# Attention and MLP in one kernel: an empty step, three moved transposes and a copy on another engine

## The chip, the cores and the metric

The kernel runs on one core of a Trainium2 chip. The metric is the device time of one execution in microseconds (us). TensorE (PE) multiplies, with its weight loads listed apart (PEld); VectorE (DVE), ScalarE (ACT) and GpSimd (POOL) do the elementwise work; SyncE (SP) and POOL issue most DMAs. Each engine works through its own list of instructions in order and waits on semaphores for the others.

## The reference

```python
q_n, k_n = rmsnorm(q, g_q), rmsnorm(k, g_k)            # 8 batches x 12 heads x 448 x 64
scores = q_n @ k_n.T / sqrt(64)
attn = softmax(scores); out = attn @ v
x = out.transpose(0, 2, 1, 3).reshape(8, 448, 768)
xn = (x - mean) / sqrt(var + 1e-6) * g_ln
y = x + relu(xn @ w_ch1) @ w_ch2                       # 768 -> 3072 -> 768
```

## The kernel before

**Units and pairs.** Heads are taken two at a time: a pair is two heads of one batch, six pairs to a batch, 48 in all (p = 0 to 47). A unit is the one or two pairs whose queries and keys are loaded and prepared together. Batch 0 has units 0 to 3, every later batch three units of two pairs; units 4, 5 and 6 are batch 1, and unit 8 is the middle unit of batch 2 (pairs 14 and 15), unit 24 the last.

**Preparing a unit** (`pieces`, line 233 on) is a set of small steps with letters. For the keys: `a` squares k on ACT (line 259) into the buffer `khl`; `d` sums the squares on DVE (line 265); `i` multiplies k by the two gains on POOL, in place (line 279); `j` (`khi`) writes the high part of k, a float16 copy, into `khl` (line 285 on POOL for the units listed in `POOL_HI`, line 287 on ACT for the others); `k` (`klo`) writes the low part, k minus the high part, on DVE (line 290). For the queries: `c` squares (ACT), `e` sums (DVE), `l` scales to float16 (DVE, line 83), `m` duplicates. From unit 7 on, SP then transposes by DMA: `x` the keys into `kU` (line 306), `y` the first 384 queries into `qU` with three DMAs (line 312), `Y` the last 64 with two (line 318). `kU`, `qU`, `qn` and `khl` have two buffers, used by even and odd units.

**Attention of a pair.** `scores(p, i)` for i = 0 to 5 multiplies 128 keys with 448 queries into a PSUM bank (line 405), and ACT takes the exponential into a tile E (line 421), which frees the bank. i = 6 is the 64 keys left over in each head; from unit 5 on the leftovers of the unit's two pairs go together into two banks with four matmuls (line 411). From pair 13 on there are three such banks. `values(p, i)` multiplies E with v into `oA` (line 458, three matmuls) and `oB` (line 460). Both lie in one set of PSUM banks, so the values of a pair begin only when `evac_o` of the pair before has divided and copied `oA` and `oB` out: two reciprocals and the products on lines 475 and 480, all on DVE.

**The MLP of a batch** runs while the attention of the next one does. First the activations `xn` of a tile of 128 tokens (DVE, line 662) are transposed by DMA from SP (line 688, `xnT`; only batch 0 uses PE), then PE multiplies with w1 (line 796, tile psH), ACT applies the relu (line 799), DVE builds sums of h in float16 (line 802), and PE multiplies with w2 (line 819). Batch 0 has an MLP of its own (`first_mlp`), whose second product is line 728 (tile psC), ends with an addition on DVE (line 755) and is stored by SP (line 954).

**The order is written out.** A hand-made list `ORDER` covers the work up to the end of batch 0's attention. Behind it `attention()` makes a list of steps, seven for each pair (p, i): in a step come the preparation steps due there (`todo`, from the tables `EARLY`, `TRANS_AT` and `PLAN`), one score, and one value product of the pair before. A step in which nothing happens isn't kept. `TRANS_AT[8] = (84, 85, 91)` puts `x`, `y` and `Y` of unit 8 at steps 84, 85 and 91, and step 7p + i is that of pair p. For p = 48 there are only the values of pair 47, at i = 1 to 6 (i = 1 has two of them). `run_rest` walks through the MLP of batch b in chunks of six matmuls or three, and behind each half chunk it emits as many steps as keep the share of steps done equal to the share of the MLP's cost, until the steps of the batch's stretch (`mark`) are used up. Then it emits `ln_list` of the next batch one item for each chunk: A, N0, N1 (lines 656 and 662), X0, X1 (line 688), R, with the X items held back until ten chunks are left. Stores of batch 0 either go out where the addition is emitted (`store`) or are put on the list `late` and go out at the next call of `store_late`.

Of the kernel before, what the change touches and what calls it, by code (L numbers as in the profile page):

```python
# [18 lines left out]
B, H, S, D = 8, 12, 448, 64  # L19
DM, FF = 768, 3072  # L20
NDC, NFF = DM // 128, FF // 128
NPAIR = H // 2
# [2 lines left out]
PAIR_UNIT = [(u, w) for u, (_, _, m) in enumerate(UNITS) for w in range(m)]  # L25
UNIT_PAIR = [PAIR_UNIT.index((u, 0)) for u in range(len(UNITS))]
EXP_BIAS = -4.0
DVE_KG, POOL_HI, POOL_DUP, ACT_Q = (0, 6), (1, 2, 3, 4, 5, 6), (3, 4, 5, 6), (0, 2, 4, 5)
POOL_SQUARE, POOL_LO = ((2, 1), (4, 0), (6, 0)), (5, 6)


# [4 lines left out]
ORDER = """  # L36
# [55 lines left out]
class _Fast:  # L92
# [446 lines left out]

    def attention(self):  # L540

        n, nu, nb0, done = B * NPAIR, len(UNITS), NPAIR, set(ORDER)
        todo = {}
        for u in range(4, nu):
            p, m = UNIT_PAIR[u], UNITS[u][2]
            if u == 4:
                continue
            plan = [(7 * (p - 4) + x, y) for x, y in PLAN]
            if u in EARLY:
                st, e = EARLY[u]  # L550
                names = ["bai", "d", "c", "e", "j", "gz", "k", "l", "m"]
                if u > 7:
                    names = NAMES[u]
                plan = [(st + (e - st) * x // 9, y) for x, y in enumerate(names)]
                if u >= DMA_UNIT:
                    plan += zip(TRANS_AT[u], "xyY")
            for at, names in plan:
                if self.late_v(u):
                    names = names.replace("z", "")
                todo.setdefault(at, []).extend(  # L560
                    self.prep_ops(u)[y] for y in names if y + str(u) not in done)
                for y in set(names) & set("kl"):
                    x = u, "qk"[y == "k"]
                    i = RING.index(x) + 3 if x in RING else nu * 2
                    if i < len(RING):
                        todo.setdefault(at + (LOAD_AT[y == "l"] if u not in EARLY else 1), []).append(
                            lambda x=RING[i]: self.load_unit(x[0], ("qk".index(x[1]),)))
        for g, at in enumerate(W2_AT):
            todo.setdefault(at, []).append(lambda g=g: self.load_w2(g))
        steps, mark = [], [0]  # L570

        for p in range(nb0, n + 1):
            for i in range(7):
                c = []
                if i == 0 and p < n and p % NPAIR == 0 and p > nb0:
                    c.append(lambda b=p // NPAIR: self.batch(b))
                c += todo.pop(7 * p + i, [])
                if p < n and f"S{p}.{i}" not in done and i < 6:
                    c.append(lambda p=p, i=i: self.scores(p, i))
                if p > nb0:  # L580
                    for x in {0: (), 1: (0, 1)}.get(i, (i,)):
                        if f"V{p - 1}.{x}" not in done:
                            c.append(lambda p=p, x=x: self.values(p - 1, x))
                if p < n and i == 6 and f"S{p}.6" not in done:
                    c.append(lambda p=p: self.scores(p, 6))
                if p > nb0 + 1 and i == 1 and (p - 1) % NPAIR:
                    c.append(lambda p=p: self.stats(p - 2))
                if p + 1 < UNIT_PAIR[DMA_UNIT]:
                    if i == 2 and f"K{p + 1}" not in done:
                        c.append(lambda p=p: self.trans_k(p + 1))  # L590
                    if i == 4 and f"Q{p + 1}" not in done:
                        c.append(lambda p=p: self.trans_q(p + 1))
                if p > nb0 and p % NPAIR == 0 and i == 6:
                    c.append(lambda p=p: self.stats(p - 1))
                if c:
                    steps.append(c)
            if p > nb0 and p % NPAIR == 0:
                mark.append(len(steps))
        return steps, mark
# [108 lines left out]
    def first_mlp(self):  # L708

        nc, sh = self.nc, self.sh  # L710
        tiles, xnT, hT, cur = self.tok_tiles(0), self.xnT, self.hS, {}

        def up(f, i):
            if i == 0:
                cur["h"] = self.ps_m.tile([128, 512], FP32, tag="mlp", name="psH")
            ps = cur["h"]
            for dc in range(3 * i, 3 * i + 3):
                nc.tensor.matmul(ps[:, 0:384], sh.w1[:, dc, ts(f, 128)], xnT[:, dc],  # L718
                                 start=(dc == 0), stop=(dc == NDC - 1))
            if i:  # L720
                nc.scalar.activation(out=hT[:, f], in_=ps[:, 0:384], func=AFT.Relu)

        def down(t, g, s):
            if s == 0:
                cur["ps"] = self.ps_m.tile([128, 512], FP32, tag="mlp", name="psC")
            ps = cur["ps"][:, 0:HCOL]
            for f in range(3 * s, 3 * s + 3):
                nc.tensor.matmul(ps, hT[:, f, ts(t, 128)], sh.w2[:, f, ts(g, HCOL)],
                                 start=(f == 0), stop=(f == NFF - 1))
            if s == 7:  # L730
                self.add(0, t, g, ps)
                if g and t < 2:
                    self.late.append((0, t, slice(0, DM)))
                elif t == 2:
                    self.store(0, t, slice(g * HCOL, g * HCOL + HCOL))
            elif s == 3:
                self.store_late()

        for f in range(UP_FIRST, NFF):
            yield 6 * 384 / 2.4, [lambda f=f, i=i: up(f, i) for i in range(2)]  # L740
        for g in range(2):
            for t in range(3):
                for s in range(4):
                    yield 6 * HCOL / 2.4, [lambda t=t, g=g, s=s: down(t, g, s)
                                           for s in (2 * s, 2 * s + 1)]
# [228 lines left out]
    def run_rest(self):  # L974
        steps, mark, upto = self.steps, self.mark, self.upto
        for b in range(B):
            tail = TAIL[b]
            chunks = list(self.mlp_chunks(b))
            total = sum(c for c, _ in chunks)
            if b + 1 == B:  # L980
                for i, (_, emit) in enumerate(chunks):
                    if i == len(chunks) - 55:
                        self.tc.mark_branch_hint_location("general", "LikelyTaken", [ENG.PE, ENG.DVE, ENG.SP, ENG.Activation, ENG.Pool])
                    for call in emit if isinstance(emit, list) else [emit]:
                        call()
                    if i in FLAG_AT:
                        self.flag(FLAG_AT.index(i))
                break
            start, goal = self.pos, mark[b + 1]
            done, items = 0.0, None  # L990
            if b == 0:
                ops, last = self.weight_sums()
            elif b == 1:
                ops += last
            left = sum(c > 0 for c, _ in chunks)
            for cost, emit in chunks:
                if not cost:
                    emit()
                    continue
                for i, call in enumerate(emit):  # L1000
                    call()
                    if i + 1 < len(emit):
                        upto(int(min(goal, start + (goal - start) * (done + cost / 2) / (total - 960 * tail))))
                left -= 1
                if (left < 10 if b == 0 else b == 1) and ops:
                    ops.pop(0)()
                done += cost
                upto(int(min(goal, start + (goal - start) * done / (total - 960 * tail))))
                if self.pos >= goal:
                    if items is None:  # L1010
                        items = self.ln_list(b + 1)
                        for u, (x, _, _) in enumerate(UNITS):
                            if x == b + 2 and self.late_v(u):
                                self.ln[f"Z{u}"] = self.prep_ops(u)["z"]
                                items.append(f"Z{u}")
                    if items and (items[0][0] != "X" or left <= DOWN):
                        x = items.pop(0)
                        self.ln[x]()
            for x in items:
                self.ln[x]()  # L1020
            if b + 2 == B:
                upto(len(steps))
# [223 lines left out]
```

## Time and profile before

The median of three runs is 584.49 us (583.91 to 585.04). One further execution was profiled.

| | |
|---|---|
| profiled execution, its own time | 584.28 us |
| its span, first to last instruction | 582.7 us |
| busy: PE, DVE, ACT, POOL | 563.3, 379.9, 376.0, 190.4 us |
| share of the span: PE, DVE, ACT, POOL | 97%, 65%, 65%, 33% |

The profile page gives the busy time of each engine and its groups of instructions by source line. The trace behind it gives each instruction's start and duration in a timeline, where the bracket at the end of a row is the engine's idle time before it and what ended it. Matmuls are pipelined: one starts long before the end of the one in front of it, so a lost stretch of PE is read from the distance between starts, and the idle time in the bracket is the smaller figure. An instruction of SP that issues a DMA ends when the issue is done, not when the data have landed.

### The profile page before, as it was taken

What the parts mean: (1) busy time and instruction counts of PE and PEld (TensorE: products, weight loads), DVE (VectorE), ACT (ScalarE), POOL (GpSimd) and SP (SyncE); (2) the same over time, 40 slices, a digit from 0 to 9 for tenths busy, and PEclk for the clock granted to TensorE, in tenths of its full rate; (3) what the DMA queues carried; (4) which work ended last, traced back from release to release, by engine and by line L of the source; (5) the groups of instructions that cost most, each with busy time, mean ns of one, the idle gap of its engine ahead of it and who ended that gap; (6) DMA issues with size and microseconds to landing.
All of it is one profiled execution on the core that took longest, in us unless ns stands there. A gap on an engine that the chain in (4) does not pass through costs nothing.

```text
span 582.7 us, 13655 instructions
## 1 busy us (share of the span) xinstructions
PE 563.3 (97%) x5446; PEld 414.2 (71%) x5446; DVE 379.9 (65%) x826; ACT 376.0 (65%) x691; POOL 190.4 (33%) x207
## 2 busy tenths in 40 slices
PE   6888999999999999999999999999999999999996
PEld 4656666677686867777677867777687777778684
DVE  6989567699657566846667586854756733663424
ACT  4998787458774779558776588747787477323130
POOL 4885635303430711553240520653141410020000
PEclk9899999999999999999999999999999999999999
DMA  7999999959672966968573887958743490030201
GB/s 198 255 238 222 219 201 162 183 170 122 121 129 79 157 136 133 133 142 112 120 119 41 187 121 137 128 152 115 145 57 64 126 104 1 2 108 1 83 2 58
DMA packets 178329, 72.59 MB, mean 125 GB/s; under 512 B 138212, under 2 KB 173220, under 8 KB 178260
## 3 DMA queue, kind: packets, MB, share of 16 engines
q1 hardware_dynamic: 133876, 52.52, 43.5%
q0 software_dynamic: 43440, 18.52, 26.5%
q8 instruction: 44, 0.72, 0.5%
q10 hardware_dynamic: 944, 0.62, 0.4%
q14 instruction: 25, 0.20, 0.1%
HBM read 52.76 MB, written 11.01 MB: 109 GB/s over the span
## 4 chain that ended last, share of the span: by engine, by line
PE 78%; DVE 7%; DMA 5%; ACT 5%; issue 2%; SPq 2%; ACTq 0%; DVEq 0%
PE psH L796 32%; PE psP L819 28%; PE psS L405 7%; PE oA L458 4%; ACT E L421 3%; PE psH L718 2%; DMA q<-in_q_dram 2%; DMA w2s<-in_k_dram 1%; PE oB L460 1%; PE psS L411 1%; DVE ssq L265 1%; DVE stat L641 1%; DMA k<-in_k_dram 1%; ACT khl L259 1%; SPq L154 1%
## 5 line engine op out<-in xcount | busy, mean ns | idle before, releaser
L421 ACT ACTIVATE E<-psS,rr_all 128x448 f16<-128x448 f32 x336 | 203.7, 635 | 41.0 <-PE psS L405 36.9
L796 PE MATMUL psH<-xnT,w 128*128 128x256 f16 (+1 forms) x2016 | 225.8, 261 | 0.4 <-DMA xnT<-xn 0.4
L796 PEld LDWEIGHTS <-w 128*128 128x128 f16 x2016 | 172.6, 98 | 24.5 <-issue 4.7
L799 ACT ACTIVATE hS<-psH 128x512 f16<-128x512 f32 x150 | 90.1, 600 | 95.9 <-PE psH L796 91.9
L819 PEld LDWEIGHTS <-hS 128*128 128x128 f16 x1080 | 99.7, 98 | 58.2 <-DVE hS L802 1.5
L819 PE MATMUL psP<-w,hS 128*128 128x384 f16 x672 | 126.8, 326 | 0.0
L405 PE MATMUL psS<-qU,kU 128*128 128x448 f16 x288 | 101.4, 354 | 5.1 <-ACT E L421 3.3
L458 PEld LDWEIGHTS <-E 128*128 128x128 f16 x1008 | 70.5, 98 | 36.8 <-issue 3.0
L279 POOL TENSOR_TENSOR k<-k,gprod 128x896 f32<-128x896 f32 x18 | 38.3, 2128 | 148.1 <-ACT khl L259 131.6
L802 DVE TENSOR_TENSOR hS<-hS 128x512 f16<-128x512 f16 (+1 forms) x119 | 58.7, 500 | 22.3 <-ACT hS L799 20.8
L819 PE MATMUL psP<-w2s,hS 128*128 128x384 f16 (+1 forms) x408 | 70.2, 321 | 0.0
L458 PE MATMUL oA<-v,E 128*128 128x65 f16 x864 | 67.1, 193 | 1.5 <-DVE x L475 0.7
L755 DVE SCALAR_TENSOR_TENSOR x<-psP,rs_all,x 128x384 f32<-128x384 f32 x60 | 36.4, 617 | 41.8 <-PE psP L819 41.1
L460 PE MATMUL oB<-v,E 128*128 128x65 f16 x288 | 51.9, 193 | 0.3
L830 POOL TENSOR_TENSOR x<-x,hS 128x384 f32<-128x384 f32 x21 | 23.5, 1128 | 83.2 <-ACT hS L898 82.6
L216 POOL DMA_DIRECT2D v<-in_v_dram x54 | 41.4, 779 | 9.1 <-PE oB L460 8.1
L473 DVE RECIPROCAL rec_all<-oA 128x6 f32<-128x6 f32 x48 | 9.2, 192 | 46.9 <-PE oA L458 46.8
L290 DVE TENSOR_TENSOR khl<-k,khl 128x896 f16<-128x896 f32 x18 | 19.6, 1088 | 29.4 <-ACT khl L287 29.4
L898 ACT ACTIVATE hS<-hS,rs_all 128x384 f32<-128x384 f32 x27 | 14.6, 604 | 33.4 <-DVE hS L802 33.4
L405 PEld LDWEIGHTS <-kU 128*128 128x128 f16 x288 | 28.1, 98 | 11.1 <-issue 2.4
L460 PEld LDWEIGHTS <-E 128*128 128x128 f16 x336 | 32.4, 97 | 0.4 <-DVE xl L480 0.4
L265 DVE TENSOR_REDUCE ssq<-khl 128x14 f32<-128x896 f32 (+1 forms) x24 | 25.5, 1061 | 5.0 <-ACT khl L259 4.8
(146 smaller groups left out, 627.2 us busy)
## 6 DMA issues: line engine op xcount, KB each, us to landing
k<-in_k_dram SPq DMA_DIRECT2D x19, 384.0 KB, 4.1
q<-in_q_dram SPq DMA_DIRECT2D x18, 384.0 KB, 3.9
out_dram<-x SPq DMA_DIRECT2D x14, 384.0 KB, 3.0
w<-in_moe_w_ch_dram POOLq DMA_DIRECT2D x3, 1536.0 KB, 15.0
v<-in_v_dram POOLq DMA_DIRECT2D x54, 64.0 KB, 4.7
out_dram<-x POOLq DMA_DIRECT2D x9, 384.0 KB, 2.7
w<-in_moe_w_ch_dram POOLq DMA_DIRECT2D x1, 2304.0 KB, 22.7
w<-in_moe_w_ch_dram POOLq DMA_DIRECT2D x2, 1152.0 KB, 14.9
```

The costliest lines, as they stand in the source:

```text
L216: nc.gpsimd.dma_start(out[:, :, j, 0:D], main[:, :, j])
L265: nc.vector.tensor_reduce(out=c["ssq"][:, n], in_=c["sq", n], axis=AX.X, op=ALU.add)
L279: (nc.vector if u in DVE_KG else nc.gpsimd).tensor_tensor(out=c["t"][1], in0=c["t"][1], in1=sh.gprod.unsqueeze(1).broadcast_to([128, g, D] ...
L405: nc.tensor.matmul(ps[0][:, 0:S], c["main"][:, ts(i, 128)], c["q"][:, ts(h, S)], start=True, stop=True)
L421: nc.scalar.activation(out=o, in_=x[:, 0:S], func=AFT.Exp, scale=self.units[u][3][:, g:g + 1], bias=EXP_BIAS)
L458: nc.tensor.matmul(oA[:, t, cs], E[:, ts(t, 128)], rhs, start=(i == 0 and t == 0), stop=(i == 6 and t == 2))
L460: nc.tensor.matmul(oB[:, cs], E[:, 320:448], rhs, start=(i == 0), stop=(i == 6))
L755: self.nc.vector.scalar_tensor_tensor(out=x, in0=ps, scalar=self.rs[:, b, t:t + 1], in1=x, op0=ALU.mult, op1=ALU.add)
L796: nc.tensor.matmul(ps[:, i], sh.w1[:, dc, ts(f + i, 128)], self.xnT[:, dc, 256 - N:256], start=(i == 0 and dc == 0), stop=(i == k - 1 and ...
L799: nc.scalar.activation(out=hT[:, f:f + k], in_=ps, func=AFT.Relu)
L802: nc.vector.tensor_tensor(out=out, in0=a, in1=c, op=op)
L819: nc.tensor.matmul(bank[x][:, c], a[:, f], w[:, f, c], start=(start and f == 0), stop=(stop and f == HALF - 1))
```

## The change

Four edits.

1. `POOL_HI` takes in units 8 to 24: their high parts of the keys are written by POOL (line 285), directly behind the product of line 279 on the same engine, and no longer by ACT (line 287).
2. The three query transposes `y` of unit 8 leave step 85 and become an item of `ln_list(1)`, behind X1.
3. The first half of the store of batch 0's third token tile goes on the list `late`.
4. In the list of steps, (p, i) = (48, 0) is kept although it is empty, so the last stretch, which is spread over the MLP of batch 6, has one step more.

```diff
-DVE_KG, POOL_HI, POOL_DUP, ACT_Q = (0, 6), (1, 2, 3, 4, 5, 6), (3, 4, 5, 6), (0, 2, 4, 5)
+DVE_KG, POOL_HI, POOL_DUP, ACT_Q = (0, 6), (1, 2, 3, 4, 5, 6, *range(8, 25)), (3, 4, 5, 6), (0, 2, 4, 5)
...
-        n, nu, nb0, done = B * NPAIR, len(UNITS), NPAIR, set(ORDER)
+        n, nu, nb0, done = B * NPAIR, len(UNITS), NPAIR, set(ORDER) | {"y8"}
...
-                if c:
+                if c or p == n:
                     steps.append(c)
...
                 if g and t < 2:
                     self.late.append((0, t, slice(0, DM)))
+                elif t == 2 and not g:
+                    self.late.append((0, t, slice(0, HCOL)))
                 elif t == 2:
-                    self.store(0, t, slice(g * HCOL, g * HCOL + HCOL))
+                    self.store(0, t, slice(HCOL, DM))
...
                         items = self.ln_list(b + 1)
+                        if b == 0:
+                            items.insert(items.index("X1") + 1, "y8")
+                            self.ln["y8"] = self.prep_ops(8)["y"]
```

## The prediction

> **What bounds the kernel now.** I read the page first, then the busy times by stretch, then TensorE's waits and its timeline around each of them.
>
> ```profile
> PE 563.3 (97%) x5446; PEld 414.2 (71%) x5446; DVE 379.9 (65%) x826; ACT 376.0 (65%) x691; POOL 190.4 (33%) x207
> 84.00:570.00 486.00, 484.05 (x4613) 358.00 (x4612) 307.23 (x683) 308.07 (x557) 135.79 (x147) 1.00 0.66 109
> ```
>
> The second row is a stretch of the span: its length, the busy time of PE, PEld, DVE, ACT and POOL, then the granted clock, 1.00 of full. In the 486 us from 84 to 570, where all of the change lies, PE is busy for 484.05. PE's order of work sets the time there, and nothing can be won but its few waits, 486.00 - 484.05 = 1.95 us counted as idle. Idle time understates them, since a matmul's span runs on while the next should already have started, so I take them again from the distances between starts. These rows, picked from PE's timeline, show them, each beside the same pair of rows elsewhere without a wait.
>
> ```profile
> 107.85 10.90 PE L728 MATMUL psC<-w,hS 128*128 128x384 f16 x66
> 119.10 1.47 PE L796 MATMUL psH<-xnT,w 128*128 128x256 f16 x12 [0.35 <-DMA xnT<-xn]
> 206.43 0.22 PE L460 MATMUL oB<-vl,E 128*128 128x130 f16 x1
> 206.58 0.57 PE L411 MATMUL psS<-qU,kU 128*64 128x448 f16 x4
> 208.93 0.25 PE L458 MATMUL oA<-v,E 128*128 128x65 f16 x3
> 209.25 0.19 PE L460 MATMUL oB<-v,E 128*128 128x65 f16 x1
> 210.08 0.25 PE L458 MATMUL oA<-v,E 128*128 128x65 f16 x3
> 210.17 0.19 PE L460 MATMUL oB<-v,E 128*128 128x65 f16 x1
> 220.57 0.22 PE L460 MATMUL oB<-vl,E 128*128 128x130 f16 x1
> 221.03 0.91 PE L411 MATMUL psS<-qU,kU 128*64 128x448 f16 x4 [0.24 <-ACT E L421]
> 342.93 0.19 PE L460 MATMUL oB<-v,E 128*128 128x65 f16 x1
> 354.35 0.22 PE L460 MATMUL oB<-vl,E 128*128 128x130 f16 x1
> 355.06 0.90 PE L411 MATMUL psS<-qU,kU 128*64 128x448 f16 x4 [0.49 <-ACT E L421]
> 493.87 0.82 PE L796 MATMUL psH<-xnT,w 128*128 128x256 f16 x6
> 494.52 0.33 PE L458 MATMUL oA<-vl,E 128*128 128x130 f16 x3
> 494.75 0.82 PE L796 MATMUL psH<-xnT,w 128*128 128x256 f16 x6
> 495.94 0.26 PE L458 MATMUL oA<-v,E 128*128 128x65 f16 x3 [0.38 <-DVE x L475]
> 496.27 0.20 PE L460 MATMUL oB<-v,E 128*128 128x65 f16 x1
> ```
>
> At 119.10 the MLP of batch 1 waits for its transposed activations: the 66 matmuls before it end at 118.75, and 0.35 us are idle. They follow each other every 10.90 / 66 = 0.165 us, so the next should have started at about 118.75 - 0.33 + 0.165 = 118.58, if one lasts 2 x 0.165: 0.52 us lost. At 209.25 `oB` follows `oA` after 0.32 us where 0.09 is usual (210.08 to 210.17): 0.23 lost. The row at 342.93 is the same place two batches on, and I take the same 0.23 for it. At 221.03 the leftover scores start 0.46 after their predecessor, not 0.15 (206.43 to 206.58), and take 0.91, not 0.57: 0.31 + 0.34 = 0.65 lost. At 355.06 it is 0.71 and 0.90: 0.56 + 0.33 = 0.89. At the end of the attention `oA` starts 1.19 after the six matmuls before it, not 0.65 (493.87 to 494.52), and `oB` 0.33 after `oA`, not 0.09: 0.54 + 0.24 = 0.78. Together 0.52 + 0.23 + 0.23 + 0.65 + 0.89 + 0.78 = 3.30 us.
>
> **The transposes of unit 8 (edit 2).** What is late at 119.10 is SP's queue. Rows of SP, then one of DVE, the line on landing from the view of the `xnT` transposes, and one of PE:
>
> ```profile
> 109.17 4.85 SPq L312 DMA_TRANSPOSE qU<-qn  x3
> ...
> 114.75 2.57 SPq L688 DMA_TRANSPOSE xnT<-xn  x2
> 120.59 2.44 SPq L318 DMA_TRANSPOSE qU<-qn  x2
> 112.53 1.01 DVE L662 SCALAR_TENSOR_TENSOR xn<-x,stat,gln 128x768 f16<-128x768 f32 x1
> DMA to landing us min/median/max: 2.7/2.8/7.5
> 130.36 0.35 PE L405 MATMUL psS<-qU,kU 128*128 128x448 f16 x1
> ```
>
> The second `xn` tile is ready at 113.54, but SP issues the two `xnT` transposes only from 114.75, behind the three of unit 8. With those gone from the front, the store of 0.5 us goes out at once, X0 follows when its tile is written, and X1 can be issued at about 113.6. From issue to landing these transposes take 2.8 us in the middle: landed at 116.4, 2.2 us before PE asks. Even 4.9 us would do, so the whole 0.52 is won; 7.5, the longest of the run, would land at 121.1, lose 2.5 and win nothing. What goes back: the three issues are the same, 4.85 us, behind X1 and a store, so about 115.4 to 120.3. Two stores and the last two query transposes of unit 8 follow, from about 121.4 and not 120.59, issued by 123.8, landed two or three us later. Their first reader is pair 14's first score, at 130.36. The slack is over 3 us, and the q loads queued behind on SP move by the same 0.8 us. Edit 3 emits a store later, but in the order of SP's instructions it stands where it stood, ahead of X0: nothing.
>
> **The high parts on POOL (edit 1).** Removed: 17 ACT instructions; added: 17 on POOL of the same shape. The fourth line below groups who waited for line 287, in us and times.
>
> ```profile
> L287 ACT ACTIVATE khl<-k x17: 934/950/981, 94.2 to 443.8; 128x896 f16<-128x896 f32 x17
> L285 POOL CAST khl<-k x2: 929/936/942, 35.5 to 63.2; 128x896 f16<-128x896 f32 x2
> L285 POOL CAST khl<-hS x1: 1555/1555/1555, 52.2 to 52.2; 128x896 f16<-128x896 f32 x1
>   DVE khl L290: 29.4, 12
> 219.50 0.95 ACT L287 ACTIVATE khl<-k 128x896 f16<-128x896 f32 x1
> 220.34 1.16 ACT L421 ACTIVATE E<-psS,rr_all 128x448 f16<-128x448 f32 x2
> 354.38 1.16 ACT L421 ACTIVATE E<-psS,rr_all 128x448 f16<-128x448 f32 x2
> 201.26 2.08 POOL L279 TENSOR_TENSOR k<-k,gprod 128x896 f32<-128x896 f32 x1 [1.46 <-ACT khl L259]
> 205.42 1.09 DVE L290 TENSOR_TENSOR khl<-k,khl 128x896 f16<-128x896 f32 x1 [1.47 <-ACT khl L287]
> 208.90 0.29 DVE L480 TENSOR_TENSOR xl<-oB,rec_all 64x128 f32<-64x128 f32 x1
> ```
>
> ACT loses 17 x 0.950 = 16.2 us of work that stands in its queue between exponentials. At 221.03 the leftover scores need two free banks, and the two exponentials that free them run from 220.34 to 221.50, right behind a high part of 0.95. Without it they run 0.9 earlier, to 220.6, and PE would ask for the two banks at 220.72 and 220.93. At 355.06 the pair ends at 355.54, so at 354.6, against 354.50 and 354.71. Both waits should go, the second with 0.1 us to spare: 0.65 + 0.89 = 1.54.
>
> POOL gains 17 x 0.936 = 15.9 us and stands idle for two thirds of the span. There the copy starts right behind the product that it reads, while ACT came to it later in its queue. DVE waited 29.4 us in all, in 12 of the 17 units, for ACT's copies, and the low part follows earlier nearly everywhere. At 205.42 DVE had been idle for 1.47, and its backlog is what makes the evacuation end at 209.19 (208.90 + 0.29) and PE lose 0.23 at 209.25. POOL's product of that unit ends at 203.34; a copy of 0.94 behind it ends at 204.3, and 1.56, the longest row of this kind, at 205.0. Either way the evacuation is done 0.4 us or more earlier, and the loss needs 0.23: both places won, 0.46.
>
> The bounds of the copy are 0.93 and 1.56 us. I take 0.94, where two of the three shown lie. What stands behind it on POOL are v loads for pairs many us ahead, products that wait for ACT anyway, and the joins of the MLP, which wait for ACT.
>
> One row speaks against moving work to POOL:
>
> ```profile
> 132.08 2.11 POOL L279 TENSOR_TENSOR k<-k,gprod 128x896 f32<-128x896 f32 x1 [19.63 <-ACT khl L259]
> 132.15 2.32 DVE L802 TENSOR_TENSOR hS<-hS 128x512 f16<-128x512 f16 x1
> 202.26 1.70 DVE L802 TENSOR_TENSOR hS<-hS 128x512 f16<-128x512 f16 x2
> ```
>
> A float16 sum of DVE that starts just behind a product on POOL lasts 2.32 us and ends 0.28 after it, while two such sums take 1.70 together at 202.26. With a copy behind each product the time in which DVE can be held grows by 0.94 for a unit. The Trainium skill, "SBUF — State Buffer", section "Who interferes with whom", has the rule: a DVE instruction with two SBUF inputs contends with a GpSimd instruction that reads SBUF, and whoever comes second is blocked for the whole instruction. The row agrees with it. In the sum I count nothing for this: around 203.4, where such a sum stands right behind the product, DVE had 1.47 us of idle time to give, and the other bound is the rival below.
>
> **The empty step (edit 4).** The values of pair 47 started six matmuls after the last ones of pair 46, while DVE needed until 496.2 to empty the banks. The last stretch now has 43 steps instead of 42, and the extra one lies just there. In the changed program's order twelve matmuls of 0.109 us stand between, so `oA` comes 0.65 later by itself and DVE is ready: 0.78 won. The price is that the 42 others shift against the MLP's chunks. In one place the last values of pair 45 and the leftover scores of the last unit then stand right behind a score, so the two free banks are asked for half a microsecond earlier. That can cost 0 to 0.65 (the loss at 221.03).
>
> **The sum.** 0.52 + 1.54 + 0.46 + 0.78 = 3.30 from 584.28, the profiled execution's own time (1.58 more than its span): 580.98. For waits that appear where the order shifted I put back 0.3, half of the 0.65 above: 581.3. The median is 0.21 above that execution: 581.5, which is 0.5% faster.
>
> **The rivals.** First, about half is won: the scores' waits stay in part, because ACT's lateness at 220 and 354 also comes from late q loads, and the last copy had only 0.1 to spare; or DVE stays late. With 1.2 to 2.0 won: 582.5 to 583.3. For it speaks the idle count, 1.95 in all; against it, that the cause of each wait is named in its row.
>
> Second, the waits move. PE runs through a fixed order, and a wait removed in front may be met again at the next late load or exponential. Then less than 1.2 is won, about 584.0. Against it speaks that outside the six places PE shows no wait from 84 to 570.
>
> Third, slower: POOL holds DVE. Place: the five of the 17 units in which DVE did not wait for the high part, so that there is no idle time to give. Price: 0.94 for each copy, all of it passed on to PE through late evacuations, 4.7 us. Time: 584.49 - 3.3 + 4.7 = 585.9. It decides once more than 3.3 us of delay reaches PE. Against it: in those units PE shows no wait for DVE now, so DVE has unseen slack. By the skill's rule alone, with every copy blocking for its whole length, it would be 17 x 0.94 = 16 us of DVE, and as many us on PE only if DVE were the bound.
>
> Fourth, the change doesn't do what it says: y8 landing too late for pair 14. It has over 3 us; 1 in 100, and part of the third.
>
> **How the numbers follow.** The forecast gets 0.70, half 0.10, no change 0.13, slower 0.07. A difference under 0.2%, 1.2 us, can't be told from no change here. So faster 0.70 + 0.10 = 0.80, the same 0.13, slower 0.07. The low end is the whole 3.30 and 0.6 more, an ACT that is less busy: 580.6. The high end takes in the first rival and part of the second, 583.6. Above it lie some 0.15, below it 0.03.
>
> **What would show it.** Right: no wait for `xnT` at 119, X0 and X1 issued by 115; no wait of the leftover scores for E near 220 and 354; DVE's wait for the high part down from 29.4 to a few us; twelve matmuls between the values of pairs 46 and 47, and PE's idle time from 84 to the end of the stretch below 0.6 us. Wrong: POOL's copies of 1.5 us and more, float16 sums of 1.4 and more behind them, and PE waiting for lines 475 and 480 at new places; a wait for E near 487.

## The result, and the profile after

The median went from 584.70 to 581.89 us (6 runs each), a ratio of 0.9948 with a 95% interval of 0.9928 to 0.9967: 2.8 us less, where 3.0 were forecast. The ratios here and below are on record with their intervals and differ a little from the quotients of the medians, here 0.9952. One of the 27 executions of the kernel before in the table below took 1176.62 us and is left out of the ratios. The profiled execution of the changed kernel took 579.58 us, its span 578.0; it is the fastest of its six runs, so below it is read for waits and not for the total.

Where the time came from is in PE's idle time. First the page's row of engines after, then the same 481 us of the span in both kernels (length, busy time of PE, PEld, DVE, ACT, POOL, granted clock, DMA share, GB/s).

```profile
PE 559.5 (97%) x5446; PEld 411.9 (71%) x5446; DVE 381.7 (66%) x826; ACT 364.4 (63%) x674; POOL 207.0 (36%) x224
```
```profile
84.00:565.00 481.00, 480.95 (x4603) 357.08 (x4602) 308.03 (x680) 295.98 (x540) 152.23 (x164) 1.00 0.65 110
```
```profile
84.00:565.00 481.00, 479.05 (x4573) 354.13 (x4572) 304.50 (x677) 306.28 (x554) 135.79 (x147) 1.00 0.67 110
```

PE has the same 5446 matmuls and is as full as before, 97%. The first of the two stretches is the kernel after: 0.05 us idle on PE, where before (second row) there were 481.00 - 479.05 = 1.95. POOL took on 16.4 us (152.23 - 135.79); ACT gave up 10.3 (306.28 - 295.98), less than the 16.2 us of the removed rows, in part because such rows overlap their neighbours by about 0.1 us each, and in part because the faster kernel has 30 more matmuls in this window, and work of ACT with them. PE's 0.05 of idle time does not mean that nothing is lost, as the distances show. PE's timeline of the kernel after, at the places that the prediction took apart:

```profile
73.77 0.88 PE L411 MATMUL psS<-qU,kU 128*64 128x448 f16 x4
...
115.76 2.76 PE L728 MATMUL psC<-w,hS 128*128 128x384 f16 x16
118.36 1.36 PE L798 MATMUL psH<-xnT,w 128*128 128x256 f16 x11
...
130.97 0.25 PE L458 MATMUL oA<-v,E 128*128 128x65 f16 x3
131.27 0.20 PE L460 MATMUL oB<-v,E 128*128 128x65 f16 x1
...
208.30 0.25 PE L458 MATMUL oA<-v,E 128*128 128x65 f16 x3
208.39 0.19 PE L460 MATMUL oB<-v,E 128*128 128x65 f16 x1
...
219.71 0.22 PE L460 MATMUL oB<-vl,E 128*128 128x130 f16 x1
219.86 0.57 PE L411 MATMUL psS<-qU,kU 128*64 128x448 f16 x4
...
352.39 0.22 PE L460 MATMUL oB<-vl,E 128*128 128x130 f16 x1
352.54 0.57 PE L411 MATMUL psS<-qU,kU 128*64 128x448 f16 x4
...
490.87 0.33 PE L458 MATMUL oA<-vl,E 128*128 128x130 f16 x3
491.10 1.47 PE L798 MATMUL psH<-xnT,w 128*128 128x256 f16 x12
492.41 0.25 PE L458 MATMUL oA<-v,E 128*128 128x65 f16 x3
492.61 0.20 PE L460 MATMUL oB<-v,E 128*128 128x65 f16 x1
...
573.83 0.33 PE L821 MATMUL psP<-w2s,hS 128*128 128x192 f16 x2
```

At 118.36 the MLP follows the matmuls before it without a bracket. At 208.39 `oB` follows `oA` by the usual 0.09, and at 219.86 and 352.54 the leftover scores follow by 0.15 and take 0.57: nothing lost in this execution. At the end twelve matmuls stand between the values of pairs 46 and 47, and `oA` needs no wait, though `oB` follows by 0.20 and not 0.09, so 0.11 stay lost. And there is a new loss: `oB` at 131.27 comes 0.30 after `oA`, where 0.09 is usual, 0.21 us.

To have one number for each execution, I take PE's stretch from the start of the first leftover scores of unit 5 (line 411, the first row above at 73.77; 74.01 before) to the end of PE's last matmul (the last row above, 573.83 + 0.33 = 574.16; 577.81 before). It leaves out the start of the program and the last stores, neither of which the change touches.

| execution | PE stretch, us |
|---|---|
| before; a second execution | 503.81; 504.03 |
| after; a second execution | 500.39; 500.69 |

The pairs differ by 3.42 and 3.34 us. The time from PE's last matmul to the end of the span was 4.92 and 5.08 us before, 3.87 and 6.10 after. So the profiled spans, 582.7 and 578.0, differ by 4.7 us, of which 3.42 are PE's stretch, 1.05 the end of the program and the rest its start. The first profiled execution after beats its own median by 2.3 us; its end alone is 2.23 shorter than that of the second one, and that part is not of the change.

### The profile page after: what moved, and what is told of

Its sections match the earlier page's. It is cut to its first block, busy times and chain, and to the rows that moved or that the text cites. A ratio compares the mean times of both kernels' runs of the same rounds, so it can differ in the third digit from the quotient of the medians.

```text
span 578.0 us, 13670 instructions
## 1 busy us (share of the span) xinstructions
PE 559.5 (97%) x5446; PEld 411.9 (71%) x5446; DVE 381.7 (66%) x826; ACT 364.4 (63%) x674; POOL 207.0 (36%) x224
## 4 chain that ended last, share of the span: by engine, by line
PE 77%; DVE 1%; issue 0%; DVEq 0%
PE psH L798 33%; PE psP L821 30%; PE psS L405 7%; PE oA L458 4%; PE oB L460 1%; PE psS L411 1%; DVE qn L83 0%; DVE w2s L763 0%; DVE ssq L265 0%; DVE w L763 0%; DVE xn L662 0%; DVE hS L804 0%; DVE x L475 0%; DVE xl L757 0%; DVE xl L480 0%
## 5 line engine op out<-in xcount | busy, mean ns | idle before, releaser
L804 DVE TENSOR_TENSOR hS<-hS 128x512 f16<-128x512 f16 (+1 forms) x119 | 60.2, 512 | 19.3 <-ACT hS L801 17.8
L83 DVE SCALAR_TENSOR_TENSOR qn<-q,rr_all 128x256 f16<-128x256 f32 (+2 forms) x69 | 24.8, 420 | 7.2 <-ACT rr_all L269 7.1
```

Of the source, the lines that this page charges most:

```text
L804: nc.vector.tensor_tensor(out=out, in0=a, in1=c, op=op)
```

## The experiments

The repeats come first, then each edit by itself, then the cost of POOL's copies, then the new wait. The column "before" is the kernel before, run beside the experiment on the same chip; every ratio has its 95% interval, and the last column is taken from the one profile of each kernel.

| kernel | median us (runs) | before us (runs) | ratio | PE stretch |
|---|---|---|---|---|
| changed kernel | 581.89 (6) | 584.70 (6) | 0.9948 [0.9928, 0.9967] | 500.39 |
| changed kernel again | 582.00 (5) | 584.40 (15) | 0.9956 [0.9942, 0.9971] | 500.69 |
| before again | 585.5 (1) | 584.56 (25) | - | 504.03 |
| edit 1 alone | 582.63 (6) | 584.58 (27) | 0.9967 [0.9955, 0.9980] | 501.60 |
| edits 2 and 3 alone | 584.44 (10) | 584.58 (27) | 0.9995 [0.9984, 1.0006] | 503.81 |
| edit 4 alone | 584.17 (10) | 584.58 (27) | 0.9995 [0.9982, 1.0007] | 502.09 |
| edits 1 and 4 | 582.16 (10) | 584.56 (25) | 0.9965 [0.9953, 0.9976] | 500.87 |
| copies of 4 units on POOL | 583.62 (10) | 584.58 (27) | 0.9984 [0.9974, 0.9995] | 502.37 |
| copies of 6 units on POOL | 582.67 (10) | 584.56 (25) | 0.9977 [0.9962, 0.9992] | 501.56 |
| each copy twice | 584.86 (10) | 584.40 (15) | 1.0010 [0.9992, 1.0027] | 503.30 |
| idle copy behind the low part | 581.53 (10) | 584.56 (25) | 0.9962 [0.9951, 0.9973] | 500.62 |
| weight sums behind the steps | 581.81 (5) | 584.40 (15) | 0.9954 [0.9938, 0.9970] | 500.23 |

### Both kernels once more

> The changed kernel once more, beside the two above on the same chip. Theory: one wait of PE from 84 us on, near 131, 0.21 us lost; PE's last matmul about 3.4 us earlier against the score near 76 us than in the kernel before; 581.3 to 582.5 us. What the first profile had beside that, 1.1 us less between the last matmul and the end of the span, does not come again if it belongs to that one execution.

> The kernel before, profiled once more. The runs of edit 1, edit 4 and four units alone show no wait for xnT at 119 us, although unit 8's transposes stand ahead of it there. Theory: that wait belongs to executions in which the key transpose of unit 8 is issued slowly (7.1 us against 5.6 to 6.0); here it is gone if the issue takes 6.5 us or less, and the wait of oB near 131 us is there instead. Waits near 209, 343 and 496 us come again to within 0.02 us of idle time; those near 221 and 355, behind a q load, come again with other sizes. Rival: the wait at 119 comes with the order, and is there again with 0.3 us or more.

The changed kernel repeats: 582.00 us. The kernel before, run unchanged for a second profile, shows something else. Its PE timeline at the place that edit 2 aims at, and its SP timeline:

```profile
119.43 1.25 PE L796 MATMUL psH<-xnT,w 128*128 128x256 f16 x10
...
132.04 0.25 PE L458 MATMUL oA<-v,E 128*128 128x65 f16 x3
132.35 0.20 PE L460 MATMUL oB<-v,E 128*128 128x65 f16 x1
102.58 6.89 SPq L306 DMA_TRANSPOSE kU<-khl  x1
109.58 4.77 SPq L312 DMA_TRANSPOSE qU<-qn  x3
115.08 2.57 SPq L688 DMA_TRANSPOSE xnT<-xn  x2
```

The `xnT` transposes stand behind the three of unit 8, as in the first profile, and PE has no bracket at 119.43: the wait of 0.52 us that the prediction took from the first profile is not there. Instead `oB` at 132.35 follows `oA` by 0.31, the loss that I had put down to the change.

The expectation tied the wait to how long SP takes to issue the key transpose ahead of these (6.5 us or less for no wait); at 6.89 it was gone all the same, so that bound was wrong. What decides is when both sides come to meet. From the end of the second issue to the moment at which PE could ask there were 118.58 - 117.32 = 1.26 us in the first profile (117.32 = 114.75 + 2.57), and 119.43 - 117.65 = 1.78 here. The first lost 0.52, so it would have needed 1.26 + 0.52 = 1.78: this one had just that.

### Edits 2 and 3 alone

```diff
-        n, nu, nb0, done = B * NPAIR, len(UNITS), NPAIR, set(ORDER)
+        n, nu, nb0, done = B * NPAIR, len(UNITS), NPAIR, set(ORDER) | {"y8"}
...
+                elif t == 2 and not g:
+                    self.late.append((0, t, slice(0, HCOL)))
...
+                            items.insert(items.index("X1") + 1, "y8")
```

> Edits 2 and 3 alone: unit 8's query transposes behind X1, the first half store put off. Theory: the wait at 119 is gone (0.52 won), and the new wait of oB for DVE line 480 near 131 us (0.21 lost) that the changed kernel shows is there too, because PE comes 0.5 earlier to a DVE that works through the weight sums; net 0.3, about 584.4 us, not to be told from 584.7. The waits at 209, 221, 343, 355 and 496 stay. Rival: the wait near 131 comes from the copies on POOL; then it is absent here.

584.44 against 584.58 us, 0.9995 with an interval that holds 1. PE's timeline shows the loss at 131 here too, with the old ACT copies and without edit 4:

```profile
131.22 0.25 PE L458 MATMUL oA<-v,E 128*128 128x65 f16 x3
131.53 0.20 PE L460 MATMUL oB<-v,E 128*128 128x65 f16 x1
```

Edit 3 was not tried alone. In all, seven profiled executions have the transposes of unit 8 in their old place (two of the kernel before and those of edit 1, edit 4, edits 1 and 4, four units, six units). From the first leftover scores to the first matmul of batch 1's MLP PE took 44.58 or 44.59 us in six of them, and 44.57 to 44.59 in the six profiles with the transposes moved; only the first profile of the kernel before has 45.09. Edit 2 guards against a wait that one execution in seven had. By time it is worth nothing that can be measured, which edits 1 and 4 without it say as well (below).

### Edit 4 alone, and edits 1 and 4

```diff
-                if c:
+                if c or p == n:
```

> Edit 4 alone: the empty step. Theory: only the wait of the values of pair 47 goes, 0.66 to 0.78 won, about 584.0 us; all other waits stay, and none appears near 487 us where the leftover scores now stand right behind a score. Rival: the tighter order costs 0.3 or more at the leftover scores of the last unit, and 0.4 or less is left.

> Edits 1 and 4 without 2 and 3: unit 8's query transposes ahead of X0 as before. Theory (from the runs so far): in most executions the wait at 119 us is not there, and where it is gone PE meets DVE's weight sums near 131 and loses 0.21 there, so edit 2 wins 0.0 to 0.3 us: 582.0 to 582.3 us, the changed kernel's 581.9 within the noise. Rival (the prediction's sum): edit 2 is worth 0.5, 582.4 or above, with the wait at 119 in the profile.

Edit 4 alone took 584.17 us, 0.9995, which can't be told from no change; a gain of 0.66 would have been 0.9989 and lies inside the interval. Its PE stretch of 502.09 says more than it is worth, because ACT was early in that execution; its timeline on ACT and that of edit 1 alone:

```profile
217.58 0.95 ACT L259 ACTIVATE qn<-q 128x896 f32<-128x896 f32 x1 [0.74 <-DMA q<-in_q_dram]
```
```profile
217.50 0.95 ACT L259 ACTIVATE qn<-q 128x896 f32<-128x896 f32 x1 [1.56 <-DMA q<-in_q_dram]
```

ACT's square of q, which stands ahead of the exponentials in question, waits for a q load whose landing differs between executions: 0.74 us with edit 4 alone, 1.56 with edit 1 alone, 1.18 in the profile before. So the leftover scores' loss near 220 is not one number: worked out from the same distances it was 0.65 before, 0.21 with edit 4 alone and ACT's copies still in place (the scores start on time and take 0.78, not 0.57), and 0.12 with edit 1 alone.

What edit 4 is worth on PE can be read where nothing else differs between the kernels. PE's order is the same up to a matmul of line 819 at 472.04 us in the first profile before (469.05 after). From its start to the end of PE's last matmul PE took 105.76 or 105.77 us in the six profiles without edit 4 and 105.11 in the seven with it: 0.65 to 0.66 won, in every profiled execution.

Edits 1 and 4 together took 582.16 us, as the whole change does (582.00). With edit 1 alone at 582.63 the empty step is the 0.5 us between them, a difference of two medians without an interval of its own.

### Edit 1 alone

```diff
-DVE_KG, POOL_HI, POOL_DUP, ACT_Q = (0, 6), (1, 2, 3, 4, 5, 6), (3, 4, 5, 6), (0, 2, 4, 5)
+DVE_KG, POOL_HI, POOL_DUP, ACT_Q = (0, 6), (1, 2, 3, 4, 5, 6, *range(8, 25)), (3, 4, 5, 6), (0, 2, 4, 5)
```

> Edit 1 alone: the high parts of units 8 to 24 on POOL. Theory (each wait of PE has its own cause): the waits at 209, 221, 343 and 355 us are gone, those for xnT at 119 (0.35 idle) and for the evacuation at the end of the attention (0.38 idle) stay, and there is no new one. PE loses 2.0 to 2.1 us less than before (0.46 + 1.54 by the prediction's sum), so about 582.6 us against 584.7. Rival (waits move): new waits of 0.5 us and more, and less than 1.0 won, 583.7 or above.

582.63 us, 1.95 less than before, where the two terms of the prediction make 1.54 + 0.46 = 2.0. PE's only wait from 84 us on that the view of waits lists is the one at the end, which is edit 4's:

```profile
PE oA L458 <- DVE x L475: 0.4, 1, 0.4
```

The wait at 119, which the expectation kept, did not come, and `oB` near 131 lost 0.22. The kernel after shows what the copies did. The view of line 285, with durations (minimum, median, maximum, in ns) and, in its last line, who waited for it:

```profile
L285 POOL CAST khl<-k x19: 926/927/1007, 35.3 to 438.2; 128x896 f16<-128x896 f32 x19
  DVE khl L290: 10.6, 11
```

The 19 copies (17 of them new) take 0.927 us, the longest 1.007. DVE waits 10.6 us for them in 11 units, not 29.4 in 12. PE's stretch is 501.60 us, 2.21 and 2.43 less than in the two executions before.

### Which units carry edit 1

```diff
-POOL_HI = (1, 2, 3, 4, 5, 6)
+POOL_HI = (1, 2, 3, 4, 5, 6, 13, 14, 19, 20)
```

> Edit 1 for four units only, 13, 14, 19 and 20, the ones prepared just ahead of the four waits; the other 13 keep their copy on ACT. Theory: the four waits have local causes, so all four are gone and the same 2.0 us is won as with all 17 units, about 582.6 us. Rival (ACT's and DVE's backlog builds up over many units): the waits at 221 and 355 stay in part, and 1.2 us or less is won, 583.5 or above.

583.62 us: 1.0 less than before, not the 2.0 of all 17 units. That is the rival's time, but not its mechanism: the leftover scores near 220 and 354 themselves lose 0.04 us at most. The four units chosen are those next to the four places that the prediction gives to edit 1. Part of the shortfall is the q load, which was latest in this execution: ACT's square waited 1.92 us for it and PE lost 0.49 just ahead of 219.7, against 0.12 with all units. The other part lies at a new place. Timeline of this kernel on DVE and PE:

```profile
234.37 1.09 DVE L290 TENSOR_TENSOR khl<-k,khl 128x896 f16<-128x896 f32 x1 [1.44 <-ACT khl L287]
241.44 1.14 DVE L755 SCALAR_TENSOR_TENSOR x<-psP,rs_all,x 128x384 f32<-128x384 f32 x2
241.82 0.71 PE L796 MATMUL psH<-xnT,w 128*128 128x256 f16 x5
242.64 0.65 PE L819 MATMUL psP<-w,hS 128*128 128x384 f16 x3
```

At 234.37 the low part of unit 15 waits 1.44 us for ACT's copy, and DVE has not caught up 7 us later: its additions at 241.44 empty the banks that PE's `psP` matmuls take at 242.64. Five matmuls of 0.109 us should have let them start at 242.37, so 0.27 are lost. Taking in units 15 and 21 tests that:

```diff
-POOL_HI = (1, 2, 3, 4, 5, 6, 13, 14, 19, 20)
+POOL_HI = (1, 2, 3, 4, 5, 6, 13, 14, 15, 19, 20, 21)
```

> Edit 1 for units 13, 14, 15, 19, 20 and 21 alone. The run with four units lost 0.27 us at 242 us, where PE waits for an addition of DVE (line 755) that stands behind unit 15's low part, which waited 1.44 us for ACT. Theory: with unit 15 and 21 on POOL that wait is gone, and the time is that of all 17 units, 582.6 us within 0.5. Rival: more of the other eleven units matter, and it stays at 583.6.

```profile
138.80 0.76 PE L411 MATMUL psS<-qU,kU 128*64 128x448 f16 x4
...
239.77 2.46 PE L796 MATMUL psH<-xnT,w 128*128 128x256 f16 x21
242.06 0.81 PE L819 MATMUL psP<-w,hS 128*128 128x384 f16 x4
```

PE's timeline with six units: 21 matmuls of 0.109 us from 239.77 end in time for 242.06, and nothing is lost. The median is 582.67, that of edit 1 is 582.63, and the PE stretches are 501.56 and 501.60. (The ratio is the worse one, 0.9977 against 0.9967, because three of the ten runs took 583.4 to 585.1 us.) So six of the 17 units carry most of the gain, but not all of it, and the equal stretches are in part luck. The leftover scores at 138.80 take 0.76 us here and 0.57 with all 17 units, and near 186, 319 and 453 PE loses 0.10 each, by its starts, which all 17 units take away: 0.46 us together. Against that stand 0.50 that edit 1 alone lost near 220 and 354 and that this execution did not: ACT's squares of q there waited 1.56 and 1.74 us for a load with edit 1 alone, 1.25 and 0.57 with six units. That four fall short of six by their 0.95 us is not shown: the intervals overlap, and 0.31 is all that the profile ties to units 15 and 21 (0.27 here and 0.04 at the same place near 377).

### What a copy on POOL costs

```diff
-                nc.gpsimd.tensor_copy(out=c["khl"][:, :, 0], in_=c["t"][1])
+                for _ in range(2 if u > 7 else 1):
+                    nc.gpsimd.tensor_copy(out=c["khl"][:, :, 0], in_=c["t"][1])
```

> The changed kernel with each copy of a high part on POOL (units 8 to 24) made twice, one behind the other: the suspected cost doubled, 17 x 0.93 = 15.8 us more of POOL. Theory: DVE and POOL have the slack, PE's waits from 84 us on stay as in the changed kernel (one, 0.05 idle near 131), and the time is 581.9 within 0.6 us. Rival (POOL holds DVE, and it reaches PE): new waits of PE for lines 475 and 480, 1 to 4.7 us more, 583 to 586.6.

584.86 us against 582.00 of the changed kernel run beside it: 17 more copies of 0.93 us, of which 2.9 us reach the end. The whole gain of the change is gone, so the theory failed; the rival had the time right. By its starts PE loses 2.95 us that the changed kernel does not: 0.40 near 143, 0.32 or 0.33 each near 209 and 343, where `oB` waits for line 481 as the rival said (480 in the kernel before), and 0.95 each near 243 and 377, at another line. The wait of PE that the view lists for these two (total, times, longest) and the timeline on POOL, DVE and PE at the first of them:

```profile
PE psP L822 <- DVE x L758: 1.6, 2, 0.8
```
```profile
233.08 1.93 POOL L286 CAST khl<-k 128x896 f16<-128x896 f32 x2
235.04 1.09 DVE L291 TENSOR_TENSOR khl<-k,khl 128x896 f16<-128x896 f32 x1 [2.13 <-POOL khl L286]
...
242.11 1.14 DVE L758 SCALAR_TENSOR_TENSOR x<-psP,rs_all,x 128x384 f32<-128x384 f32 x2
243.31 1.46 PE L822 MATMUL psP<-w,hS 128*128 128x384 f16 x8 [0.79 <-DVE x L758]
```

It is unit 15 again: the two copies end at 235.01, DVE waits 2.13 us for them and then 7 us later its addition holds PE for 0.79. But two things grew here at once, the time that POOL works and the moment at which DVE's low part can start. The next kernel keeps the first and undoes the second: the added instruction copies k onto itself, behind the low part, where nothing on DVE waits for it.

```diff
...
+            if u > 7:
+                nc.gpsimd.tensor_copy(out=c["t"][1], in_=c["t"][1])
```

> The changed kernel with an idle copy of the unit's k onto itself on POOL behind each low part (units 8 to 24): 17 x about 0.93 us more of POOL, as in the run with each copy made twice, but nothing of DVE waits for it in its line. Theory (the 2.9 us of that run came from DVE waiting in its order for the later copy): no wait of PE for line 757 at 243 and 377 us, and 582.0 us within 0.7. Rival (POOL holds DVE's way to the memory): sums and two-input operations of DVE behind the low part last 0.5 us and more longer, the waits for line 757 are there, 584 us or above.

```profile
L293 POOL COPY k<-k x17: 924/933/2327, 97.7 to 440.8; 128x896 f32<-128x896 f32 x17
```

The added copies take 0.933 us in the middle, and the median is 581.53: no cost. How long DVE waited for the high part, in the kernel with each copy made twice (its line 291) and in this one:

```profile
  DVE khl L291: 22.2, 13
  DVE khl L290: 10.6, 11
```

Doubling the copies took that wait from 10.6 to 22.2 us, and the idle copies leave it at the 10.6 of the changed kernel. DVE's work did not grow with the doubled copies. The page's row of engines of that kernel has 381.3 us for DVE, where the changed kernel has 381.7:

```profile
PE 561.0 (96%) x5446; PEld 412.6 (71%) x5446; DVE 381.3 (65%) x826; ACT 364.2 (62%) x674; POOL 222.9 (38%) x241
```

So the 2.9 us came through DVE's queue, which waits in order for the high part, and not through POOL making DVE's instructions longer. The idle copies do not show by themselves that POOL can't do the latter, because they gave it little to hold: beside 13 of the 17 DVE ran a sum of squares (line 265), of 1.07 to 1.09 us as without them.

POOL does hold DVE, and in the changed kernel already. These are the second of two float16 sums on DVE near 203, before and after:

```profile
203.55 0.41 DVE L802 TENSOR_TENSOR hS<-hS 128x512 f16<-128x512 f16 x1
202.93 1.15 DVE L804 TENSOR_TENSOR hS<-hS 128x512 f16<-128x512 f16 x1
```

The second row runs beside POOL's copy of 202.78 to 203.79 and is 0.74 us longer. The same happens near 336; no other sum is held by a copy, and the page has 1.5 us more for the whole group of sums (58.7 before, 60.2 after). PE loses nothing behind either place: `oB` at 208.39 follows by 0.09.

### The new wait

The kernel after on DVE, around the loss at 131:

```profile
129.24 0.76 DVE L763 TENSOR_TENSOR w2s<-w,w2s 128x1152 f16<-128x1152 f16 x1
129.90 0.19 DVE L473 RECIPROCAL rec_all<-oA 128x6 f32<-128x6 f32 x1
130.92 0.29 DVE L480 TENSOR_TENSOR xl<-oB,rec_all 64x128 f32<-64x128 f32 x1
```

A sum of weights runs until 130.00, the reciprocal starts only as it ends, and line 480, which frees the bank of `oB`, ends at 131.21. PE's `oB` starts at 131.27. Emitting these sums behind the steps of their chunk and not ahead of them puts the evacuation first:

```diff
-                if (left < 10 if b == 0 else b == 1) and ops:
+                if b == 0 and left < 10 and ops:
                     ops.pop(0)()
                 done += cost
                 upto(...)
+                if b == 1 and ops:
+                    ops.pop(0)()
```

> The changed kernel with the weight sums of DVE in the MLP of batch 1 emitted behind the attention steps of their chunk instead of ahead of them. Theory: DVE's sums are what makes oB wait near 131; with one sum of 0.67 us less ahead of the evacuation the wait is gone and PE ends 0.2 us earlier than in the changed kernel, about 581.7 us. Rivals: the sums were not it and the wait stays; or the sums now come late for the products that read them and PE waits at line 821, 0.2 us or more lost.

```profile
129.41 0.18 DVE L473 RECIPROCAL rec_all<-oA 128x6 f32<-128x6 f32 x1
130.41 0.29 DVE L480 TENSOR_TENSOR xl<-oB,rec_all 64x128 f32<-64x128 f32 x1
130.74 1.43 DVE L763 TENSOR_TENSOR w2s<-w,w2s 128x1152 f16<-128x1152 f16 x2
131.14 0.25 PE L458 MATMUL oA<-v,E 128*128 128x65 f16 x3
131.23 0.19 PE L460 MATMUL oB<-v,E 128*128 128x65 f16 x1
```

The sums now stand behind line 480, and `oB` follows `oA` by 0.09. Its PE stretch, 500.23, is the shortest of all. The time, 581.81 against 582.00, is the better by a fifth of a microsecond, which these runs can't resolve.

## Why the prediction was right, and where it was not

**The time, 581.5 forecast, 581.89 and 582.00 measured.** The sum of the six places was 3.30, with 0.3 put back. The first pair of profiles differs by 3.42 on PE, the medians by 2.8 and 2.4. How PE's 3.4 become these stays open in part: only two executions of each kernel were profiled, and the time behind PE's last matmul varied by up to 2.2 us between executions of one kernel. What the 3.4 consist of can be read from the traces. The table takes at each place the distance between PE's starts, less the shortest that any of the 13 profiles has there; the times are those of the first profile before.

| PE loses, us, near | before; again | edit 1 alone | six units | after; again |
|---|---|---|---|---|
| 119, start of batch 1's MLP | 0.52; 0 | 0 | 0 | 0; 0 |
| 131, `oB` | 0; 0.22 | 0.22 | 0.22 | 0.21; 0.20 |
| 139, leftover scores | 0; 0.15 | 0 | 0.16 | 0; 0 |
| 186, 319 and 453, second product of the MLP, together | 0.28; 0.28 | 0 | 0.30 | 0; 0 |
| 209 and 343, `oB`, together | 0.46; 0.45 | 0 | 0 | 0; 0 |
| 220, up to the leftover scores | 0.62; 0.97 | 0.16 | 0 | 0; 0.29 |
| 354, up to the leftover scores | 0.97; 0.97 | 0.34 | 0 | 0; 0 |
| 243 and 377, second product of the MLP, together | 0.07; 0.08 | 0 | 0 | 0; 0 |
| from 472 on (edit 4) | 0.66; 0.66 | 0.66 | 0.65 | 0; 0 |

The second pair has no wait at 119 and differs by 3.34 all the same, because there both kernels lose the 0.2 near 131, and that execution of the kernel before lost 0.35 more near 220 and 0.15 near 139, of which the changed kernel's 0.29 near 220 takes back a part. Edit 1 also took away 0.36 us at five places of the table (186, 319, 453, 243, 377), which the prediction did not count ("outside the six places PE shows no wait"): the view of waits lists none of them as idle time. So that the sum fits is in part luck: a term of 0.52, which most executions don't have, stands in it, and these 0.36, with 0.15 near 139 in some executions, are left out.

**Edit 2: the term of 0.52 failed.** The step that failed is "so the whole 0.52 is won". The queue was read rightly, and X0 and X1 are issued early now. But the wait was a property of the one execution that had been profiled, and six of the seven profiles with the old order have none. The prediction had no rival for that; it took a single trace for the kernel. The 0.52 in the difference of the first pair is real for that pair, but the 0.21 near 131 comes in its place, so it is worth 0.31 even there; by the medians it is worth nothing that can be told from zero.

**Edit 1: right in sum, its cause right, its size not as sharp as it looked.** 2.0 forecast, 1.95 by time; on PE, 0.46 and 1.09 came from the places that were named (table, before less edit 1 alone), 0.35 from those that were not. The copies take 0.927 us, 0.94 was taken. But the waits of the leftover scores did not always go whole. With the change run again, PE's timeline has these two rows:

```profile
218.42 0.19 PE L460 MATMUL oB<-v,E 128*128 128x65 f16 x1
219.63 0.20 PE L460 MATMUL oB<-v,E 128*128 128x65 f16 x1
```

They start 1.21 apart where 0.96 or 0.97 is usual before them, so 0.25 is lost just ahead of the leftover scores, behind a square of q that had waited 1.69 us for its load. That is the first rival's mechanism, at a small size; edit 1 alone lost 0.16 near 220 and 0.34 near 354. "DVE's wait for the high part down to a few us" was wrong too: 10.6 remain, since in 11 units the low part still comes up before POOL is done, and those 10.6 us cost PE nothing that the profile shows. The gain of the wait for lines 475 and 480 near 209 and 343 came as forecast.

**Edit 4: right.** The values of pair 47 no longer wait, twelve matmuls stand ahead of them, and 0.78 - 0.11 = 0.67 is won by these rows, and 0.65 to 0.66 in every profile with the edit. No wait for E appeared near 487. The time could not show it alone.

**The allowance of 0.3** met 0.21 at 131 and 0.11 at 492.61, though not for the reason given. The place at 131 is not one where a score shifted: DVE's sums of weights end at their own time, and a PE that arrives earlier meets them. The second execution of the kernel before lost the same 0.2 there, so it belongs to a PE without the wait at 119, and not to edit 1 or 4.

**The rivals.** The second, waits that move, holds for that one place. The third named POOL holding DVE as the way to a loss. POOL's copies do hold DVE's float16 sums, but at two places and by 0.74 us each, where the rival had 0.94 in each of five units, and PE loses nothing behind either. Of its signs, no float16 sum behind a copy took 1.4 us (the one of 2.31 near 132 stands behind a product and took 2.32 before), and PE's wait for line 480 at a new place is the one near 131, which the kernel before has as well. The prediction also set 1.70 us for two sums at 202.26 beside the held one as if nothing held them; the first of the two is held too, 1.37 us beside a product that ends at 203.34, and a free one takes 0.41. A loss of about the rival's size can be made, 2.9 us with the copies doubled, and its way is the in-order wait on DVE. The Trainium skill's "SBUF — State Buffer", section "Who interferes with whom", which the prediction weighed, says that a DVE instruction with two SBUF inputs contends with a GpSimd instruction that reads SBUF. The traces agree for these sums (0.41 us free, 1.15 beside a copy); what that costs depends on the room behind it, and here there was room.

## What to carry to other kernels

When PE is full, the gain of an edit is the sum of a few named waits, and each of them is worth its size only if it is there in more than one execution: profile the kernel before twice, and drop the terms that don't repeat. Move a producer to the engine that already holds its input, and ask of the new place when the consumer in the other engine's queue can start, because here 17 copies that nobody waited for cost nothing, and 17 copies in front of a waiting queue cost 2.9 us. Before moving all instances, find those next to the waits: here six of 17 carried most of the gain. And compare place by place, not by the total: two kernels with the same total had lost it at different places.

## What the runs showed of the hardware that was not expected

SP's issue of the same transpose of keys (one instruction, line 306) took from 5.64 us (four units on POOL) to 7.77 (weight sums behind the steps) from one execution to another, 6.89 and 7.09 in the two of the kernel before. Where unit 8's transposes stand right behind it, they began at 106.97 us with the 5.64 and at 109.17 with the 7.09. ACT's wait for the same q load was 0.74 to 1.92 us. The end of the program, from PE's last matmul to the last store, took 3.87 to 6.16 us; no edit here touches it, and in the first pair of profiles it alone made 1 us of the difference.
